# Float32 sums of key tiles ahead of one product for the last two groups of an attention and two-layer kernel

## The chip, the cores and the metric

The kernel runs on one core of one Trainium2 chip. The time is device microseconds (us) of that core for one execution; lower is better. Before the change it is 417.5 us, the median of three runs (417.23 to 418.01).

## The reference

Cosine attention over 8 batches, 12 heads, 448 positions and 64 columns per head, and behind it two matrix products with a leaky ReLU between them:

```python
q_n = q / (norm(q) + 1e-06);  k_n = k / (norm(k) + 1e-06)
scores = q_n @ k_n.T / tau                  # tau = 0.1
attn = exp(scores - max);  attn = attn / (sum(attn) + 1e-09)
x = (attn @ v) laid out as (3584 tokens, 768)
h = x @ w_in                                # 768 -> 2048
out = maximum(0.01 * h, h) @ w_out          # 2048 -> 768, float32
```

The kernel leaves the maximum out, since the scores are bounded by 1/tau. The softmax denominators are column sums of the exponentials, which TensorE forms as products with ones.

## The kernel before

**Engines.** TensorE (PE) does all products and a few transposes, ScalarE (ACT) the exponentials, logarithms and the leaky ReLU, VectorE (DVE) norms, normalisation, 32x32 transposes and copies out of PSUM, GpSimd (POOL) the squares of q and k and the loads of v and of the weights, SyncE (SP) the other transfers. The order of instructions on each engine is written out by hand: an engine runs its instructions in the order in which the program records them, and waits for others through semaphores.

**Heads.** Two heads make a pair; pair s has 0 to 47. Pairs 0 to 11 (the first two batches) go through an older form with four key tiles of 128, 128, 128 and 64 rows (`key_tiles`, `totals`, `products`, `scale`). The other 36 pairs go through `UNITS`: 18 units u of two pairs, each with seven key tiles i. A key tile is made by `quad_tiles`: eight 64x32 products (line 417) that each take an eighth of the array, into two PSUM banks, and one `exp` on ACT (line 423) into a buffer `pe` of 128 x 896 bf16, kept as `pq[u, i]`. Its 896 columns are two halves of 448 queries.

**Groups.** Units are gathered into ten groups g. The last two are group 8 (units 14 and 15) and group 9 (units 16 and 17). When all its key tiles are there, a group gets three passes of `group_products(g, e)` (line 442), each 7 key tiles x 4 strips x 2 row halves = 56 products of form 64x32 with 448 columns: e = None multiplies by `ones` and gives the denominators, e = 0 and 1 multiply by v (`vq`). `group_logs` takes the logarithm of the denominators (line 451), `group_inverse` the exponential of its negative (line 454), and `group_scale` on DVE (line 467) multiplies the v products by it into `xT`.

**Visits.** The 126 key tiles run in 42 visits of three (`visits`). A visit normalises one pair to come, makes its first tile, then one of a group's three passes if one is due (`parts`), then the other two tiles, and then some items of the feed-forward work: `first` (6 products with `w_in`, line 494, and the leaky ReLU on ACT, line 505) and `second` (16 products with `w_out`, line 531, a copy to `osb` by DVE, line 541, and a store by SP). A planner (`level`, `share`) deals these items out to visits so that each has about as much TensorE work. Group 8's ones pass falls in visit 38, its v passes in visits 39 and 40; group 9's come after the last visit, 41, with feed-forward items between them.

**Preparing pairs.** For a pair s: SP loads q or k (`load_qk`), POOL squares them (line 216), DVE sums (line 232), ACT takes roots (lines 245 and 246), DVE normalises (lines 253, 254 and 260) and transposes (line 306), and SP lays the result out as `qkT` in six transfers (line 315). `hold` is a one-element copy on POOL (line 616) that keeps POOL's queue behind DVE's normalisation. In the visits, `prepare` does this for the pair in `preps`; the last pair, 47, is prepared in visit 36.

**Before the visits.** Straight-line code takes care of pairs 6 to 14 and the first feed-forward chunk. `load_w_out(0)` and `load_w_out(1)` on POOL's queue load the two column halves of `w_out`, 1536 KB each (line 110). `settle(s)` normalises and transposes a pair, holds, and has the squares of a later pair made. `attend(j)` does the denominators, the products and the scaling of one quad of the older form.

**Memory.** `ps` is all of PSUM, eight banks dealt oldest first by `banks`. `vbp` holds three `v_b` buffers and `vrb` two remainders for the older form alone; `id128` is the identity for its transposes. `pep` has 25 `pe` buffers.

Of the kernel before, what the change touches and what calls it, by code (L numbers as in the profile page):

```python
# [8 lines left out]
F32 = mybir.dt.float32  # L9
BF16 = mybir.dt.bfloat16  # L10
AF = mybir.ActivationFunctionType
ALU = mybir.AluOpType
# [4 lines left out]
def kernel(  # L17
# [10 lines left out]
    nc = tc.nc  # L28
    B, H, S, D = q.shape
# [8 lines left out]
    NSLOT = B * NPAIR  # L38
    NQ = NPAIR // 2
    KT = D_model // 128  # L40
    MT = D_ff // 128
    HALF = D_model // 2
# [5 lines left out]
    ctx.enter_context(tc.manual_schedule())  # L48
    cpool = ctx.enter_context(tc.tile_pool(name="consts", bufs=1))
    ldp = ctx.enter_context(tc.tile_pool(name="ld", bufs=4))  # L50
    vbp = ctx.enter_context(tc.tile_pool(name="vb", bufs=3))
    smp = ctx.enter_context(tc.tile_pool(name="small", bufs=3))
    qnp = ctx.enter_context(tc.tile_pool(name="qn", bufs=3))
    ttp = ctx.enter_context(tc.tile_pool(name="tt", bufs=2))
# [11 lines left out]
    gp = nc.gpsimd  # L66
# [8 lines left out]
    def banks(count, keep=None):  # L75
        lo, hi = (0, 8) if not deals["apart"] else (0, 4) if count == 2 else (4, 8)
        x = min(
            (i for i in range(lo, hi, count) if not set(range(i, i + count)) & set(kept.values())),
            key=lambda i: max(age[i : i + count]),
        )  # L80
        deals["n"] += 1
        age[x : x + count] = [deals["n"]] * count
        if keep:
            kept[keep] = x
        return ps[:, x] if count == 1 else ps[:, x : x + count]
# [12 lines left out]
    w_out_sb = cpool.tile([128, MT, D_model], BF16, name="w_out_sb")  # L98
    w_in_r = moe_w_in.rearrange("(j p e) n -> e p j n", p=128, e=2)
    w_out_r = moe_w_out.rearrange("(mo mi) n -> mi mo n", mi=128)  # L100
# [4 lines left out]
            out=w_in_sb[:, e::2, n0 : n0 + D_ff // 2], in_=w_in_r[e, :, :, n0 : n0 + D_ff // 2]  # L105
        )

    def load_w_out(half):
        n0 = half * HALF
        gp.dma_start(out=w_out_sb[:, :, n0 : n0 + HALF], in_=w_out_r[:, :, n0 : n0 + HALF])  # L110

    def main(x, b, h0, nh):
        return x[b, h0 : h0 + nh, 0:MAIN].rearrange("h (p t) d -> p h t d", t=3)
# [28 lines left out]
    def load_qk(s):  # L142
        if s >= NSLOT:
            return
        whole = ldp.tile([128, 14 * D], F32, name="qk_h")
        if s >= OLD:
            u, which = divmod(s - OLD, 2)
            for w, pair in enumerate(UNITS[u][1]):
                b, h0 = pair // NPAIR, 2 * (pair % NPAIR)
                nc.sync.dma_start(  # L150
                    out=whole[64 * w : 64 * w + 64],
                    in_=(q, k)[which][b, h0 : h0 + 2].rearrange("h (p t) d -> (h p) (t d)", t=14),
                )
            raw[s] = whole
            return
        b, h0 = s // NPAIR, 2 * (s % NPAIR)
        q_h, k_h = halves(whole)
        nc.sync.dma_start(out=q_h[:, :, 0:3], in_=main(q, b, h0, 2))
        nc.sync.dma_start(out=k_h, in_=main(k, b, h0, 2))
        for i, x in enumerate((q, k)):  # L160
            nc.sync.dma_start(
                out=q_h[64 * i : 64 * i + 64, :, 3],
                in_=x[b, h0 : h0 + 2, MAIN:S].rearrange("h p d -> p h d"),
            )
        raw[s] = (q_h, k_h)
# [3 lines left out]
    vb, vrb = {}, []  # L169

    def load_v(j):
        if j >= B * NQ:
            return
        b, jj = divmod(j, NQ)
        vb[j] = vbp.tile([128, 4, 3, D], BF16, name="v_b")
        gp.dma_start(out=vb[j], in_=main(v, b, 4 * jj, 4))

    def load_v_rem(b, heads=range(4)):
# [7 lines left out]
    GROUPS = [(6,), (7, 8), (9, 10), (11,)] + [(j, j + 1) for j in range(12, 24, 2)]  # L186
# [2 lines left out]
        (g, (2 * js[0] + x, 2 * js[-1] + x if len(js) == 2 else 2 * js[0] + 1))  # L189
        for g, js in enumerate(GROUPS) for x in range(len(js))  # L190
    ]
    vq = {}

    def load_vq(g):
# [14 lines left out]
    def squares(s, eng=gp, parts=(0, 1)):  # L209
        if s >= NSLOT:  # L210
            return
        sq = sqt[s % 3]
        if s >= OLD:
            sqs[s] = sq
            x = raw[s].rearrange("p (t d) -> p t d", d=D)
            gp.tensor_tensor(sq[:, :, :D], x, x, op=ALU.mult)  # L216
            return
        sqs[s] = halves(sq.rearrange("p t d -> p (t d)"), D + 1)
        for i in parts:
            x, y = raw[s][i], sqs[s][i]  # L220
            if eng is nc.scalar:
                nc.scalar.activation(y[..., :D], x, func=AF.Square)
            else:
                eng.tensor_tensor(y[..., :D], x, x, op=ALU.mult)  # L224
# [23 lines left out]
    qn = {}  # L248
# [83 lines left out]
    def scores(s, kis):  # L332
        key_tiles([(s, ki) for ki in kis])
# [68 lines left out]
            given_back((j, e))  # L402

    pq = {}

    def quad_tiles(which):

# [19 lines left out]
    def group_products(g, e):  # L427


        us = [u for u, (gg, _) in enumerate(UNITS) if gg == g]  # L430
        two = len(us) == 2
        po = banks(2)
        for i in range(7):
            for strip in range(4):
                for w in range(2):
                    x, a = strip // 2, strip % 2
                    rows = slice(64 * w, 64 * w + 64)
                    weights = ones[rows] if e is None else (
                        vq[g][rows, strip if two else a, i]
                        .rearrange("p (d e) -> p e d", e=2)[:, e if two else w ^ x]  # L440
                    )
                    nc.tensor.matmul(  # L442
                        out=po[32 * strip : 32 * strip + 32, w, :S],
                        lhsT=weights, rhs=pq[us[x if two else 0], i][rows, a, :],
                        start=(i == 0), stop=(i == 6),
                    )
        return po
# [5 lines left out]
    def group_inverse(g):  # L453
        nc.scalar.activation(grb[g], grb[g], func=AF.Exp, scale=-1.0)
# [108 lines left out]
    def feed_groups(c, count):  # L563
        for _ in range(count):
            work[c].pop(0)[1]()
# [22 lines left out]
    nc.vector.memset(warm, 1.0)  # L588
    ones = cpool.tile([128, 32], BF16, name="ones")
    nc.vector.memset(ones, 1.0)  # L590
    ones_rem = cpool.tile([128, 2, 32], BF16, name="ones_rem")
    nc.vector.memset(ones_rem, 0.0)
    for i in range(2):
        nc.vector.memset(ones_rem[64 * i : 64 * i + 64, i], 1.0)
    for i in range(2):
        vrb.append(cpool.tile([128, NQ, 4, D], BF16, name=f"v_rem{i}"))
        nc.vector.memset(vrb[i], 0.0)
    id128 = cpool.tile([128, 128], BF16, name="id128")
    make_identity(nc, id128)
# [15 lines left out]
    def hold(x):  # L615
        gp.tensor_copy(out=seen, in_=x)  # L616
# [157 lines left out]
    hold(qn[s + 2][:, 6, 0, 0:1])  # L774
    squares(s + 4)
    load_v(s // 2 + 1)
    load_w_out(1)
    sums(s + 3)
    feed_groups(0, 2)
    scores(s + 1, (0, 1))  # L780
# [24 lines left out]
    def settle(s, more=()):  # L805
        normalise(s)
        if s >= OLD:
            transposes(s)
        hold(qn[s][:, 6, 0, 0:1])
        for x in (*more, s + 2):  # L810
            squares(x)
# [25 lines left out]

    scores(s + 4, (2,))
    scores(s + 5, (0, 1))
    feed_groups(0, 1)  # L840
    attend(NQ + 1)
    load_qk(s + 10)
    settle(s + 7)
    sums(s + 8)

    scores(s + 5, (2, 3))
# [40 lines left out]
        for n in range(len(visits))  # L887
    ]

    held = []  # L890
    fed = 0
    for n, tiles in enumerate(visits):
        s = preps.get(n, NSLOT)
        g, e = parts.get(n, (None, None))
        scaling = e is not None

        def prepare():
            if s < NSLOT:
                transposes(s)
                load_qk(s + 4)  # L900
                hold(qn[s][:, 6, 0, 0:1])
                squares(s + 2)
                sums(s + 1)

        normalise(s)
        if not scaling:
            prepare()
        quad_tiles(tiles[:1])
        if g is not None:
            po = group_products(g, e)  # L910
            if e is None:
                group_logs(g, po)
            else:
                group_scale(g, e, po)
        if scaling:
            prepare()
        quad_tiles(tiles[1:])
        if g is not None and e is None:
            group_inverse(g)
        for u, i in tiles:  # L920
            if i == 6 and u and UNITS[u][0] != UNITS[u - 1][0]:
                load_vq(UNITS[u][0])
        for c in marked:
            if at[c] == n:
                held += marked[c]
        level = min(
            (sum(loads[c] for c in loads if at[c] <= x) - fed + sum(side[n : x + 1])) / (x - n + 1)
            for x in range(n, len(visits))
        )
        share = (level - side[n]) / (4 if n == len(visits) - 1 else 1)  # L930
        now, done = [], 0
        while held:
            w = weight(held[0][0], held[0][1][0])
            if now and done + w / 2 > share:
                break
            now.append(held.pop(0)[1][1])
            done += w
        fed += done
        for fn in now[:-1]:
            fn()  # L940
        roots(s + 1)
        for fn in now[-1:]:
            fn()
    g = len(GROUPS) - 1
    group_logs(g, group_products(g, None))
    group_inverse(g)
    rest = [fn for _, (_, fn) in held]
    cut = len(rest) // 3
    for fn in rest[:cut]:
        fn()  # L950
    for e in range(2):
        group_scale(g, e, group_products(g, e))
# [39 lines left out]
```

## Time and profile before

| what | value |
|---|---|
| median of three runs | 417.5 us (417.23 to 418.01) |
| the profiled execution, its own time | 416.43 us |
| its span, first to last instruction | 414.6 us |
| granted TensorE clock over the span | 1.000 |
| ScalarE busy | 250.2 us, 60% |
| VectorE busy | 221.5 us, 53% |
| GpSimd busy | 114.6 us, 28% |
| denominators by ones (line 442, ones) | 560 matmuls in 10 passes |
| first-layer products (line 494) | 768 matmuls, 151.1 us |
| second-layer products (line 531) | 912 matmuls, 151.3 us |

The profile is of one execution, and its times are measured from the first instruction. Groups of instructions are named by line, engine, operation and out<-in tiles. PE is the matmul row, PEld the weight loads, which overlap it. A matmul's end is modelled from its size, so the starts say more than the durations: the recorded duration of a 64x32 matmul is 349 ns while 56 of them pass in 1.32 us. The chain of waits is the work that ended last, followed back from the last instruction; each of its steps has a start, a length and what ran.

### The profile page before, as it was taken

What the parts mean: (1) busy time and instruction counts of PE and PEld (TensorE: products, weight loads), DVE (VectorE), ACT (ScalarE), POOL (GpSimd) and SP (SyncE); (2) the same over time, 40 slices, a digit from 0 to 9 for tenths busy, and PEclk for the clock granted to TensorE, in tenths of its full rate; (3) what the DMA queues carried; (4) which work ended last, traced back from release to release, by engine and by line L of the source; (5) the groups of instructions that cost most, each with busy time, mean ns of one, the idle gap of its engine ahead of it and who ended that gap; (6) DMA issues with size and microseconds to landing.
All of it is one profiled execution on the core that took longest, in us unless ns stands there. A gap on an engine that the chain in (4) does not pass through costs nothing.

```text
span 414.6 us, 11342 instructions
## 1 busy us (share of the span) xinstructions
PE 407.1 (98%) x4799; PEld 212.3 (51%) x4799; DVE 221.5 (53%) x387; ACT 250.2 (60%) x431; POOL 114.6 (28%) x149
## 2 busy tenths in 40 slices
PE   8899999999999999999999999999999999999997
PEld 3335555544555555544455555554445555654565
DVE  6977976855778556766474964464621301210022
ACT  5997876378657785668865688547764464004300
POOL 4875543433234132413331433122210000000000
PEclk9999999999999999999999999999999999999999
DMA  7999998775377851884275681742442100020022
GB/s 195 242 214 220 210 234 187 181 223 129 60 206 182 204 132 22 204 229 99 53 186 157 151 229 43 175 126 84 91 90 68 51 39 3 38 77 0 2 76 76
DMA packets 41964, 53.82 MB, mean 130 GB/s; under 512 B 12474, under 2 KB 32314, under 8 KB 41914
## 3 DMA queue, kind: packets, MB, share of 16 engines
q1 hardware_dynamic: 25738, 41.01, 35.0%
q0 software_dynamic: 15488, 11.80, 19.7%
q8 instruction: 37, 0.61, 0.6%
q10 hardware_dynamic: 688, 0.30, 0.2%
q14 instruction: 13, 0.11, 0.1%
HBM read 45.61 MB, written 11.01 MB: 137 GB/s over the span
## 4 chain that ended last, share of the span: by engine, by line
PE 87%; DMA 4%; ACT 3%; DVE 3%; POOL 2%; SPq 1%; issue 1%; POOLq 0%
PE ps L531 34%; PE ps L494 34%; PE ps L442 9%; PE ps L417 7%; ACT pe L355 2%; DMA qk_h<-in_k_dram 2%; PE ps L366 2%; DVE qn L270 1%; DMA xT<-in_k_dram 1%; DMA xT<-in_q_dram 1%; POOL sq L224 1%; PE ps L346 1%; POOL sq L216 1%; DVE ss L238 0%; SPq L131 0%
## 5 line engine op out<-in xcount | busy, mean ns | idle before, releaser
L531 PE MATMUL ps<-w_out_sb,hT 128*128 128x384 bf16 (+1 forms) x912 | 151.3, 324 | 0.3 <-DVE xT L397 0.3
L494 PE MATMUL ps<-xT,w_in_sb 128*128 128x384 bf16 (+1 forms) x768 | 151.1, 353 | 0.0
L423 ACT ACTIVATE pe<-ps 128x896 bf16<-128x896 f32 x126 | 108.9, 915 | 46.1 <-PE ps L417 46.1
L531 PEld LDWEIGHTS <-hT 128*128 128x128 bf16 x912 | 86.5, 98 | 64.3 <-issue 10.0
L494 PEld LDWEIGHTS <-w_in_sb 128*128 128x128 bf16 x768 | 72.6, 98 | 74.3 <-issue 9.7
L505 ACT ACTIVATE hT<-ps 128x384 bf16<-128x384 f32 (+1 forms) x128 | 67.4, 552 | 56.0 <-PE ps L494 55.0
L541 DVE COPY osb<-ps 128x384 f32<-128x384 f32 (+1 forms) x57 | 31.2, 548 | 100.7 <-PE ps L531 100.6
L216 POOL TENSOR_TENSOR sq<-qk_h 128x896 f32<-128x896 f32 x36 | 61.0, 1695 | 9.2 <-DMA qk_h<-in_k_dram 7.7
L616 POOL CAST seen<-qn 128x1 f32<-128x1 bf16 x46 | 8.5, 185 | 169.4 <-DVE qn L260 160.5
L260 DVE TENSOR_TENSOR qn<-qk_h,r 128x896 bf16<-128x896 f32 x36 | 42.4, 1176 | 1.2
L232 DVE TENSOR_REDUCE ss<-sq 128x14 f32<-128x910 f32 x36 | 38.0, 1054 | 1.1 <-POOL sq L216 1.1
L355 ACT ACTIVATE pe<-ps 128x896 bf16<-128x896 f32 x42 | 35.9, 917 | 1.8 <-PE ps L346 1.7
L417 PE MATMUL ps<-qkT 64*32 64x448 bf16 x1008 | 36.5, 353 | 0.0
L253 DVE TENSOR_REDUCE r<-norms 128x14 f32<-128x28 f32 x48 | 8.6, 178 | 48.3 <-ACT norms L246 47.7
L467 DVE TENSOR_TENSOR xT<-ps,rb 128x448 bf16<-128x448 f32 x32 | 18.4, 617 | 23.2 <-PE ps L442 21.5
L306 DVE STREAM_TRANSPOSE tt<-qn 128x448 f32<-128x448 f32 x36 | 29.6, 821 | 0.9
L442 PE MATMUL ps<-pe,vq 64*32 64x448 bf16 x1008 | 27.0, 349 | 0.0
L245 ACT ACTIVATE ss<-ss 128x14 f32<-128x14 f32 x48 | 10.3, 214 | 25.4 <-DVE ss L232 24.4
L417 PEld LDWEIGHTS <-qkT 64*32 64x32 bf16 x1008 | 13.1, 91 | 19.2 <-issue 14.5
L442 PEld LDWEIGHTS <-vq 64*32 64x32 bf16 x1008 | 14.5, 92 | 8.0 <-issue 0.3
L442 PE MATMUL ps<-pe,ones 64*32 64x448 bf16 x560 | 15.1, 349 | 0.0
L346 PE MATMUL ps<-qkT 64*64 64x448 bf16 (+1 forms) x132 | 12.9, 359 | 2.1 <-ACT pe L355 1.2
(53 smaller groups left out, 218.9 us busy)
## 6 DMA issues: line engine op xcount, KB each, us to landing
qk_h<-in_q_dram SPq DMA_DIRECT2D x36, 224.0 KB, 4.0
qk_h<-in_k_dram SPq DMA_DIRECT2D x36, 224.0 KB, 4.3
out_dram<-osb SPq DMA_DIRECT2D x20, 384.0 KB, 2.3
qkT<-tt SPq DMA_DIRECT2D x72, 56.0 KB, 3.3
qkT<-tt SPq DMA_DIRECT2D x36, 112.0 KB, 3.5
vq<-in_v_dram POOLq DMA_DIRECT2D x16, 224.0 KB, 5.0
w_in_sb<-in_moe_w_in_dram POOLq DMA_DIRECT2D x4, 768.0 KB, 11.2
w_out_sb<-in_moe_w_out_dram POOLq DMA_DIRECT2D x2, 1536.0 KB, 22.3
```

Of the source, the lines that this page charges most:

```text
L216: gp.tensor_tensor(sq[:, :, :D], x, x, op=ALU.mult)
L232: nc.vector.tensor_reduce(ss[s], sqs[s], axis=AX.X, op=ALU.add)
L260: nc.vector.tensor_tensor(qn[s].rearrange("p m d e -> p m e d"), raw[s].rearrange(f"p ({t[1:-1]} d) -> p m e d", e=n, d=D), r.rearrange(f" ...
L306: nc.vector.transpose(out=to.rearrange(("p g (c m) -> p m g c", "p g (m c) -> p m g c")[which], m=7), in_=qn[s].bitcast(F32).rearrange("p ...
L355: nc.scalar.activation(out=dst, in_=sc[:, :, :S], func=AF.Exp, scale=inv_tau)
L417: nc.tensor.matmul(out=sc[32 * strip : 32 * strip + 32, a, :S], lhsT=x[rows, c0 : c0 + 32], rhs=x[rows, 0:S], start=True, stop=True,)
L423: nc.scalar.activation(out=pq[u, i], in_=sc[:, :, :S], func=AF.Exp, scale=inv_tau)
L442: nc.tensor.matmul(out=po[32 * strip : 32 * strip + 32, w, :S], lhsT=weights, rhs=pq[us[x if two else 0], i][rows, a, :], start=(i == 0), ...
L494: nc.tensor.matmul(out=pm[:, :n], lhsT=w_in_sb[:, kt, m * 128 : (m + 1) * 128], rhs=xT[c // 2][:, kt, c0 : c0 + n], start=(done + i == 0), ...
L505: nc.scalar.activation(out=hT[c][:, m, :n], in_=pm[:, :n], func=AF.Prelu, alpha=0.01)
L531: nc.tensor.matmul(out=po2[:, : hi - lo], lhsT=hT[c][:, m, ts * 128 : (ts + 1) * 128], rhs=w_out_sb[:, m, half * HALF + lo : half * HALF + ...
L541: nc.vector.tensor_copy(out=o[:, cols], in_=po2[:, : hi - lo])
```

## The change

Four edits stand in the diff.

1. For groups 8 and 9, the seven key tiles of each unit are added up element by element into one float32 tile of 128 x 896 (`whole[u]`), six additions a unit. GpSimd does unit 14, VectorE units 15, 16 and 17 (`add_up`). The ones pass of these two groups is then eight products of float32 `whole[u]` with float32 ones (`ones_f`) in place of 56 with bf16. VectorE's additions of a visit stand behind the visit's first feed-forward item; GpSimd's stand ahead of that visit's `hold` and `squares`. `group_inverse` of group 9 moves behind the first feed-forward item after its ones pass.
2. Two tiles of sums need room: `v_b` and `vrb` become views of one tile `shared`, whose space the sums take over once the older form is through with it, and `ones_f` is written over `id128` ahead of the visits.
3. The second half of `w_out` is loaded in two transfers of eight row blocks each.
4. Before the visits, the normalising, transposing and holding of pair 13, the load of pair 16 and the squares of pair 15 move ahead of one feed-forward item and `attend(NQ + 1)`, and with them their six `qkT` transfers on SP.

```diff
@@ -48,7 +48,6 @@
     ctx.enter_context(tc.manual_schedule())
     cpool = ctx.enter_context(tc.tile_pool(name="consts", bufs=1))
     ldp = ctx.enter_context(tc.tile_pool(name="ld", bufs=4))
-    vbp = ctx.enter_context(tc.tile_pool(name="vb", bufs=3))
     smp = ctx.enter_context(tc.tile_pool(name="small", bufs=3))
     qnp = ctx.enter_context(tc.tile_pool(name="qn", bufs=3))
     ttp = ctx.enter_context(tc.tile_pool(name="tt", bufs=2))
@@ -105,9 +104,13 @@
             out=w_in_sb[:, e::2, n0 : n0 + D_ff // 2], in_=w_in_r[e, :, :, n0 : n0 + D_ff // 2]
         )
 
-    def load_w_out(half):
-        n0 = half * HALF
-        gp.dma_start(out=w_out_sb[:, :, n0 : n0 + HALF], in_=w_out_r[:, :, n0 : n0 + HALF])
+    def load_w_out(half, pieces=1):
+        n0, step = half * HALF, MT // pieces
+        for m in range(0, MT, step):
+            gp.dma_start(
+                out=w_out_sb[:, m : m + step, n0 : n0 + HALF],
+                in_=w_out_r[:, m : m + step, n0 : n0 + HALF],
+            )
 
     def main(x, b, h0, nh):
         return x[b, h0 : h0 + nh, 0:MAIN].rearrange("h (p t) d -> p h t d", t=3)
@@ -172,7 +175,7 @@
         if j >= B * NQ:
             return
         b, jj = divmod(j, NQ)
-        vb[j] = vbp.tile([128, 4, 3, D], BF16, name="v_b")
+        vb[j] = v_old[:, j % 3]
         gp.dma_start(out=vb[j], in_=main(v, b, 4 * jj, 4))
 
     def load_v_rem(b, heads=range(4)):
@@ -189,6 +192,8 @@
         (g, (2 * js[0] + x, 2 * js[-1] + x if len(js) == 2 else 2 * js[0] + 1))
         for g, js in enumerate(GROUPS) for x in range(len(js))
     ]
+    ADDED = len(GROUPS) - 2
+    BY_VECTOR = len(UNITS) - 3
     vq = {}
 
     def load_vq(g):
@@ -402,6 +407,20 @@
             given_back((j, e))
 
     pq = {}
+    whole, due, summed = {}, [], set()
+
+    def add_up(eng):
+        for u, i in list(due):
+            if (gp if u < BY_VECTOR else nc.vector) is not eng:
+                continue
+            if i == 1:
+                if UNITS[u - 2][0] >= ADDED and UNITS[u - 2][0] not in summed:
+                    return
+                whole[u] = sum_of[u % 2]
+            due.remove((u, i))
+            eng.tensor_tensor(
+                whole[u], pq[u, 0] if i == 1 else whole[u], pq[u, i], op=ALU.add
+            )
 
     def quad_tiles(which):
 
@@ -430,6 +449,16 @@
         us = [u for u, (gg, _) in enumerate(UNITS) if gg == g]
         two = len(us) == 2
         po = banks(2)
+        if e is None and g >= ADDED:
+            summed.add(g)
+            for strip in range(4):
+                for w in range(2):
+                    rows = slice(64 * w, 64 * w + 64)
+                    nc.tensor.matmul(
+                        out=po[32 * strip : 32 * strip + 32, w, :S], lhsT=ones_f[rows],
+                        rhs=whole[us[strip // 2]][rows, strip % 2, :], start=True, stop=True,
+                    )
+            return po
         for i in range(7):
             for strip in range(4):
                 for w in range(2):
@@ -588,12 +617,19 @@
     nc.vector.memset(warm, 1.0)
     ones = cpool.tile([128, 32], BF16, name="ones")
     nc.vector.memset(ones, 1.0)
+    shared = cpool.tile([128, 3840], BF16, name="shared")
+    v_old = shared[:, :2304].rearrange("p (j h t d) -> p j h t d", j=3, t=3, d=D)
+    sum_of = [
+        shared[:, 1792 * i : 1792 * (i + 1)].bitcast(F32).rearrange("p (a c) -> p a c", c=S)
+        for i in range(2)
+    ]
     ones_rem = cpool.tile([128, 2, 32], BF16, name="ones_rem")
     nc.vector.memset(ones_rem, 0.0)
     for i in range(2):
         nc.vector.memset(ones_rem[64 * i : 64 * i + 64, i], 1.0)
     for i in range(2):
-        vrb.append(cpool.tile([128, NQ, 4, D], BF16, name=f"v_rem{i}"))
+        lo = 2304 + 768 * i
+        vrb.append(shared[:, lo : lo + 768].rearrange("p (j g d) -> p j g d", g=4, d=D))
         nc.vector.memset(vrb[i], 0.0)
     id128 = cpool.tile([128, 128], BF16, name="id128")
     make_identity(nc, id128)
@@ -774,7 +810,7 @@
     hold(qn[s + 2][:, 6, 0, 0:1])
     squares(s + 4)
     load_v(s // 2 + 1)
-    load_w_out(1)
+    load_w_out(1, 2)
     sums(s + 3)
     feed_groups(0, 2)
     scores(s + 1, (0, 1))
@@ -837,10 +873,13 @@
 
     scores(s + 4, (2,))
     scores(s + 5, (0, 1))
+    normalise(s + 7)
+    transposes(s + 7)
+    load_qk(s + 10)
+    hold(qn[s + 7][:, 6, 0, 0:1])
+    squares(s + 9)
     feed_groups(0, 1)
     attend(NQ + 1)
-    load_qk(s + 10)
-    settle(s + 7)
     sums(s + 8)
 
     scores(s + 5, (2, 3))
@@ -887,19 +926,23 @@
         for n in range(len(visits))
     ]
 
+    ones_f = id128.bitcast(F32)[:, 0:32]
+    nc.vector.memset(ones_f, 1.0)
     held = []
     fed = 0
     for n, tiles in enumerate(visits):
         s = preps.get(n, NSLOT)
         g, e = parts.get(n, (None, None))
         scaling = e is not None
+        adding = [(u, i) for u, i in tiles if i and UNITS[u][0] >= ADDED]
 
         def prepare():
             if s < NSLOT:
                 transposes(s)
                 load_qk(s + 4)
-                hold(qn[s][:, 6, 0, 0:1])
-                squares(s + 2)
+                if not adding:
+                    hold(qn[s][:, 6, 0, 0:1])
+                    squares(s + 2)
                 sums(s + 1)
 
         normalise(s)
@@ -915,6 +958,11 @@
         if scaling:
             prepare()
         quad_tiles(tiles[1:])
+        due += adding
+        add_up(gp)
+        if adding and s < NSLOT:
+            hold(qn[s][:, 6, 0, 0:1])
+            squares(s + 2)
         if g is not None and e is None:
             group_inverse(g)
         for u, i in tiles:
@@ -936,17 +984,22 @@
             now.append(held.pop(0)[1][1])
             done += w
         fed += done
-        for fn in now[:-1]:
+        for fn in now[:1]:
+            fn()
+        add_up(nc.vector)
+        for fn in now[1:-1]:
             fn()
         roots(s + 1)
-        for fn in now[-1:]:
+        for fn in now[1:][-1:]:
             fn()
     g = len(GROUPS) - 1
     group_logs(g, group_products(g, None))
-    group_inverse(g)
     rest = [fn for _, (_, fn) in held]
     cut = len(rest) // 3
-    for fn in rest[:cut]:
+    for fn in rest[:1]:
+        fn()
+    group_inverse(g)
+    for fn in rest[1:cut]:
         fn()
     for e in range(2):
         group_scale(g, e, group_products(g, e))
```

## The prediction

> **What bounds the kernel now.** I read the page's busy shares first, then the chain of waits around the two ones passes, then what the other engines wait for there.
>
> ```profile
> PE 407.1 (98%) x4799; PEld 212.3 (51%) x4799; DVE 221.5 (53%) x387; ACT 250.2 (60%) x431; POOL 114.6 (28%) x149
> ...
> 314.36 0.31 PE ps L417 x8
> 314.67 1.32 PE ps L442 x56
> 315.99 0.38 PE ps L417 x16
> ...
> 334.41 9.86 PE ps L494 x60
> 344.27 1.45 PE ps L442 x56
> 345.71 4.01 PE ps L494 x24
> ```
>
> The first line gives busy us, share and count by engine; the others are steps of the chain (start, length, what). TensorE is at 98%, and from about 80 us to 411 us every step of the chain is a TensorE step, each beginning where the last one ended. So TensorE's own instruction time sets the end: a microsecond taken out of its stream or put into it is a microsecond of span. The two L442 steps shown are the ones passes of groups 8 (visit 38) and 9 (after visit 41).
>
> How do 56 matmuls pass in 1.32 us? Three stretches of group 9's ones pass, with the matmuls in flight in brackets behind the PE busy time:
>
> ```profile
> 344.19:344.23 0.04, 0.03 (x8) 0.03 (x10) 1.00 0.00 0
> ...
> 344.23:344.39 0.16, 0.16 (x8) 0.10 (x16) 1.00 0.00 0
> ...
> 344.39:344.43 0.04, 0.04 (x16) 0.03 (x8) 1.00 0.00 0
> ```
>
> Eight start within 0.04 us; for the next 0.16 us none starts; then eight more start within 0.04 us. The eight of a round sit on eight different parts of the array and run side by side. The ninth needs the first one's part, waits until that is free, and everything recorded behind it waits too. A round, or wave, costs 1.32 / 7 = 0.189 us.
>
> **The float32 product.** This is the term that decides. Per group 56 matmuls go, 7 waves, 1.32 us. Eight float32 products come. The built program holds 4719 matmuls and 4719 weight loads where the old one holds 4799 of each: 80 fewer, so the 112 bf16 matmuls that went were replaced by 32. Each of the 16 float32 products has become two weight loads and two matmuls, recorded one behind the other, on the same part of the array, and only then comes the next product's part.
>
> No float32 matmul is in the trace, so its cost is bounded. The nearest row is the wave of 0.189 us for 448 columns. If a float32 matmul cost one wave and all eight parts ran side by side, a pass would be near 0.19 us (a gain of 1.13 a group); if every one of the 16 matmuls ran alone and took two waves, it would be 16 x 0.378 = 6.05 us (a loss of 4.73 a group). I take two waves for one matmul: an element has twice the bits, and two matmuls that are to give the full product of halves times halves must each cover both halves of the moving side, so 0.378 us. And I take the order from the windows above: the second matmul of a product finds its part taken by the first and holds back all behind it; when it starts, the next product's first one, on another part, starts right behind it. So there is one step of 0.378 us per product and one more at the end: 9 x 0.378 = 3.40 us. Against 1.32 us that is +2.08 us a group, **+4.16 us** for two. The second weight load of a product is taken as hidden behind its first matmul, as 98 ns loads are behind the 163 ns matmuls of L531; if it isn't, 16 x 0.093 us (the recorded load of a 64x32 part) adds 1.5 us.
>
> The Trainium skill, "FP8 and Floating Point Precision", section TensorE Precision Notes, says that true FP32 takes four passes through the array; two matmuls of two waves are these four, and no run here shows it yet. The skill's "TensorEngine Tiling (Array Packing)", section Key Properties, says that different tiles can execute weight loads and matmuls in parallel. By that rule alone the eight products would overlap in full, 4 x 0.189 = 0.76 us a pass, and the sum would be a gain of 1.13 us in place of the loss; the rounds of eight above agree with it only for parts that are called in turn, which these are not.
>
> **The additions.** VectorE gets 18, GpSimd 6, each over 128 x 896. The nearest rows:
>
> ```profile
> L216 POOL TENSOR_TENSOR sq<-qk_h 128x896 f32<-128x896 f32 x36 | 61.0, 1695 | 9.2 <-DMA qk_h<-in_k_dram 7.7
> ...
> L260 DVE TENSOR_TENSOR qn<-qk_h,r 128x896 bf16<-128x896 f32 x36 | 42.4, 1176 | 1.2
> ...
> 333.83 0.56 DVE L541 COPY osb<-ps 128x384 f32<-128x384 f32 x1 [1.90 <-PE ps L531]
> 351.30 2.41 DVE L467 TENSOR_TENSOR xT<-ps,rb 128x448 bf16<-128x448 f32 x4 [16.92 <-PE ps L442]
> ```
>
> At 1.18 us, VectorE's are 18 x 1.18 = 21.2 us, at 1.70 us GpSimd's 6 x 1.70 = 10.2 us. Off the path, if they end before the product that reads them. Group 9: unit 17's six additions stand behind the copy at 333.83, so 334.39 + 6 x 1.18 = 341.5, against the product at 344.27: 2.8 us to spare, and VectorE had 16.9 us idle there. Group 8: its last addition, tile (15, 6), stands behind the copy that starts at 311.79, so it ends at 312.35 + 1.18 = 313.5 against 314.67, 1.1 us to spare. Queued behind the additions on VectorE are `osb` copies and `group_scale`; TensorE meets those only when it wants their banks back, and a copy of three additions' length (3.5 us) later is still inside a visit of 5 to 7 us. On GpSimd the additions of unit 14 wait for the exponentials of visits 33 and 34 and push two squares and one load of v back by some 5 us: squares of pair 46 would end at about 286 instead of 282, and the sums that read them ran at 291.10; the load of v has some 17 us left. Cost 0; without this cover it is a wait at the products, priced as a rival.
>
> **The rest.** The ring of 25 `pe` buffers, `shared` and `ones_f` cost TensorE nothing: their earlier readers are long done. `group_inverse` behind one more activation (0.49 us) still ends some 3 us before the scaling at 351.30. One short memset joins VectorE at 80 us.
>
> ```profile
> PEld L531 <- DMA w_out_sb<-in_moe_w_out_dram: 0.7, 1, 0.7
> ...
> 70.49 5.38 PE L531 MATMUL ps<-w_out_sb,hT 128*128 128x384 bf16 x32 [0.26 <-DVE xT L397]
> ```
>
> The second half of `w_out` is issued at 49.12 and lands in some 21 us, just when line 531 wants it at 70.49. The weight load waits for this transfer, so the 0.26 us of idle TensorE is its work (the bank that the matmul takes was copied out at 67.94). In two transfers, the first piece of 768 KB lands far earlier (`w_in`'s of that size take 11.2 us), and the second one is wanted 8 matmuls, 1.3 us, later. That takes out **-0.26 us**; for 0.4 us more of issue on GpSimd, ahead of a `hold` that sat idle 1.88 us. It can cost something only if the second piece lands 1.3 us later than the whole did.
>
> Pair 13's preparation moves ahead of a feed-forward copy and of `attend`'s scaling. Its roots are there at 66.33, so VectorE normalises and transposes until 68.7, copies until 69.3 and still reaches the scaling, which waits for ACT until 69.82: cost 0. On SP the six `qkT` transfers (3.77 us of issue) pass ahead of pair 16's load, which goes from 63.26 to about 72.6; with the 7 us that loads took there it lands at about 80, 3 us later than GpSimd's squares of it began (76.67), while the sums that read them began at 83.71. Cost 0. The gain is that pair 13's `qkT` lands about 4 us earlier than its use at 80.95: cover, not time.
>
> **The sum.** +4.16 - 0.26 = **+3.9 us** on the profiled execution's 416.43 us (span 414.6 and 1.8 around it): 420.3. The median of the runs is 1.07 above that execution, so **421.4 us**.
>
> **Rivals.**
> - *All eight parts overlap* (the other side, faster): if a product's second matmul queued at its own part and let others pass, a pass would be four waves, 0.76 us, and two save 1.13. With the 0.26: -1.39, 416.1 us. For it: eight parts do run side by side. Against it: nothing started in the 0.16 us shown although the ninth alone lacked its part. It decides as soon as two passes take less than 2.9 us together.
> - *One wave each, in that order*: 9 x 0.189 = 1.70 us a pass, +0.76 - 0.26 = +0.5, 418.0 us. For it: a bf16 matmul of 448 columns costs that. Against: twice the bits.
> - *Nothing overlaps*: 6.05 us a pass, +9.46 - 0.26 = +9.2, 426.7 us. For it: no float32 matmul of this form is in the trace, and its weight loads might block all parts.
> - *Late additions*: they hold the product of group 9 from (344.27 - 334.39) / 6 = 1.65 us each on. At 2.16 us, GpSimd's slowest square, six end at 347.4: up to 3 us on top, 424.4. Against: VectorE's row is 1.18.
>
> **Chances.** The forecast (3.4 us a pass, weights hidden or not) 0.57, full overlap 0.27, one wave each 0.05, nothing overlaps 0.08, late additions 0.03. About 0.2%, 0.84 us, is what a measurement can tell from no change; full overlap is faster by more, one wave each is within it, the others are slower: 0.27, 0.05, 0.68. The forecast's own range is 420.3 to 423.0 (the 1.5 us of weight loads on top). The range runs from a little below full overlap, 415.6, to 423.0; it leaves out the case without overlap and the worst of the late additions.
>
> **What would show it.** In the chain, the two float32 passes at 3.4 us each, 16 matmuls in steps of about 0.38 us: right. At 0.8 us: the order on the array was misread. At 6 us: no overlap. The additions should be near 1.2 us on VectorE and 1.7 us on GpSimd, with no TensorE wait for either. The wait on `w_out` at 70 us should be gone. An idle gap of TensorE ahead of a float32 product, or new waits on `qkT` near 81 us, would make the additions or the moves the story instead.

## The result, and the profile after

The changed kernel takes 418.31 us (median of 22 runs, 417.31 to 420.95) against 417.23 for the one before (22 runs). The ratio is 1.0021 with a 95% interval of 1.0011 to 1.0031: slower by 0.9 us, not by the 3.9 us that were forecast. The profiled execution took 418.29 us, with a span of 416.5 us against 414.6.

The page's first line, and the chain of waits around the two float32 passes (line 457; lines 436, 523 and 560 are the former 417, 494 and 531):

```profile
PE 407.3 (98%) x4719; PEld 211.4 (51%) x4719; DVE 240.0 (58%) x406; ACT 250.2 (60%) x431; POOL 126.0 (30%) x156
...
315.73 0.31 PE ps L436 x8
316.04 0.75 PE ps L457 x16
316.79 0.38 PE ps L436 x16
...
324.20 0.77 issue
324.98 0.56 DVE osb L570
325.54 0.04 issue
325.58 0.48 PE ps L436 x7
...
336.78 9.86 PE ps L523 x60
346.63 0.91 PE ps L457 x16
347.55 4.01 PE ps L523 x24
```

The float32 passes did not get longer, they got shorter: 0.75 us instead of 1.32, and 0.91 instead of 1.45. But in visit 39 a step of VectorE has come into the chain, where every step had been TensorE's. VectorE's order there shows why:

```profile
319.98 0.56 DVE L570 COPY osb<-ps 128x384 f32<-128x384 f32 x1 [3.66 <-PE ps L560]
320.46 1.08 DVE L421 TENSOR_TENSOR shared<-pe 128x896 f32<-128x896 bf16 x1
321.57 3.48 DVE L421 TENSOR_TENSOR shared<-shared,pe 128x896 f32<-128x896 f32 x3
324.98 0.55 DVE L570 COPY osb<-ps 128x384 f32<-128x384 f32 x1
```

Unit 16's sums take over unit 14's space, so its first addition has to wait for group 8's pass in visit 38, and then four additions stand in a row. The copy behind them starts at 324.98; before, the same copy started at 321.71, 2.5 us behind the one ahead of it instead of 5.0. TensorE's tiles of visit 39 want that bank. The same copy before, and the start of visit 39's tiles and of its first feed-forward item in the chain before:

```profile
321.71 0.56 DVE L541 COPY osb<-ps 128x384 f32<-128x384 f32 x1 [1.97 <-PE ps L531]
```

```profile
321.68 0.31 PE ps L417 x8
...
323.69 5.31 PE ps L531 x32
```

There is a second loss, much earlier. Here are the waits of TensorE after 48 us (in total, times, longest), then GpSimd's order at the two transfers of `w_out`'s second half (start, length, engine, line, what, and in brackets the idle time before), then its squares before:

```profile
PE ps L436 <- DVE osb L570: 1.1, 1, 1.1
PE ps L289 <- DVE qn L275: 0.6, 1, 0.6
PE ps L351 <- DVE qkT L330: 0.4, 1, 0.4
```

```profile
48.24 0.90 POOL L110 DMA_DIRECT2D w_out_sb<-in_moe_w_out_dram  x1
53.07 0.87 POOL L110 DMA_DIRECT2D w_out_sb<-in_moe_w_out_dram  x1 [3.93 <-DVE qkT L330]
53.94 0.20 POOL L652 CAST seen<-qn 128x1 f32<-128x1 bf16 x1
54.08 1.82 POOL L229 TENSOR_TENSOR sq<-qk_h 128x512 f32<-128x512 f32 x2
```

```profile
52.31 1.82 POOL L224 TENSOR_TENSOR sq<-qk_h 128x512 f32<-128x512 f32 x2
```

GpSimd stood still for 3.9 us ahead of the second transfer, so the squares behind it began at 54.08 instead of 52.31, and sums, roots and normalisation of pair 11 came after them. (The view names VectorE's copy of `qkT` as what ended this wait, since that came last by the profile; the second experiment shows that it was something else.) TensorE waited 0.6 us for its transpose at 58 us and 0.4 us for `qkT` at 62 us.

Added up over the two profiled executions, by when the same step begins: 1.4 us later by line 560's item at 71.86 (70.49 before), 0.57 won in visit 38, 1.56 lost in visit 39 (from the start of its tiles to its first feed-forward item 3.58 us instead of 2.02), 0.54 won at group 9's pass: +1.4 - 0.57 + 1.56 - 0.54 = +1.85, the span's 1.9. Single executions differ by more than the effect (before: 416.27 to 419.89), so sizes below are ratios of runs, and the trace says only where.

### The profile page after: what moved, and what is told of

It is laid out like the page before. It is cut to its first block, busy times and chain, and to the rows that moved or that the text cites. A ratio compares the mean times of both kernels' runs of the same rounds, so it can differ in the third digit from the quotient of the medians.

```text
span 416.5 us, 11224 instructions
## 1 busy us (share of the span) xinstructions
PE 407.3 (98%) x4719; PEld 211.4 (51%) x4719; DVE 240.0 (58%) x406; ACT 250.2 (60%) x431; POOL 126.0 (30%) x156
## 4 chain that ended last, share of the span: by engine, by line
PE 92%; ACT 3%; DVE 2%; POOL 1%; issue 1%; DVEq 0%; POOLq 0%
PE ps L523 35%; PE ps L560 35%; PE ps L471 8%; PE ps L436 7%; PE ps L371 2%; ACT pe L360 2%; PE ps L641 2%; PE ps L351 2%; PE ps L289 1%; DVE qn L275 1%; DVE qkT L330 0%; PE ps L457 0%; POOL sq L221 0%; POOL sq L229 0%; DVE ss L243 0%
## 5 line engine op out<-in xcount | busy, mean ns | idle before, releaser
L265 DVE TENSOR_TENSOR qn<-qk_h,r 128x896 bf16<-128x896 f32 x36 | 43.8, 1218 | 1.2
L421 DVE TENSOR_TENSOR shared<-shared,pe 128x896 f32<-128x896 f32 x15 | 16.3, 1088 | 1.2
```

What stands on the lines that cost most here:

```text
L265: nc.vector.tensor_tensor(qn[s].rearrange("p m d e -> p m e d"), raw[s].rearrange(f"p ({t[1:-1]} d) -> p m e d", e=n, d=D), r.rearrange(f" ...
```

## The experiments

Five questions: does the early loss come from the two transfers, does the loss in visit 39 come from the additions in a row, does the move of pair 13 do anything, how does TensorE let eight float32 products overlap, and what does the float32 form still cost.

**One transfer again**, in the changed kernel.

```diff
-    load_w_out(1, 2)
+    load_w_out(1)
```

> The changed kernel with the second half of w_out in one transfer again, all else kept. Theory (the second of the two transfers waits on GpSimd for the landing of the first half of w_out, 3.9 us, and holds back the squares of the next pair): the two TensorE gaps between 57 and 63 us go (1.8 us) and the wait of 0.3 us at line 531's first use of the second half comes back, so about 1.4 us less than the changed kernel: near 416.9 us, ratio to before 0.999. Rival (the gaps come from the moved preparation of pair 13 or from the shared tile): no better than the changed kernel, 418.3, and the gaps stay.

Measured: 416.64 us, ratio to before 0.9982 (0.9972 to 0.9992). The gaps at 58 and 62 us are gone; the wait of 1.1 us in visit 39 stays. But no wait on `w_out` came back at 70 us, which the theory had counted on; the runs on the move, below, take that up.

**The two transfers alone**, in the kernel before.

> The kernel before with nothing but the two transfers for the second half of w_out. Theory (semaphore wait of the second transfer): GpSimd idle near 4 us ahead of it, TensorE 1.4 us later after 70 us, about 418.6 us, ratio 1.0035. Rival (the moved preparation or the shared tile is the cause): 0.3 us gained, about 417.0 us, ratio 0.999.

Measured: 418.0 us, ratio 1.0013 (1.0004 to 1.0023): slower, with neither sums nor move in it, though less than expected. Its wait of GpSimd is named outright:

```profile
POOL w_out_sb L111 <- DMA w_out_sb<-in_moe_w_out_dram: 2.4, 1, 2.4
```

The second transfer waits for another transfer of `w_out`: its first half. In the built program, and in the traces, GpSimd's loads take eight semaphores in turn, and the second transfer's turn falls on the one that `load_w_out(0)` has still to raise. In the changed kernel's trace that first half was issued at 29.44 us and landed at 52.79. In the three traces with the stall (the changed kernel, this one, and the one with two additions below) the second transfer starts 0.28 us after that landing: 53.07 after 52.79, 53.88 after 53.60, 53.28 after 53.00. The wait is 2.4 us here and 3.9 there, since in this execution TensorE sat idle for 1.35 us at 20 us already and GpSimd arrived later; so the loss differs from one execution to the next. The loss is also smaller here because, without the move, the two transfers still have a wait on `w_out` to take out: this trace has none at 70 us, where the kernel before has one. That share was not measured by itself. VectorE's copy of `qkT`, named above, is not what the transfer waits for: here and with two additions it ends 0.5 to 0.7 us after the transfer has started.

**At most two additions in a row**, in the changed kernel.

```diff
-    def add_up(eng):
+    def add_up(eng, most=99):
         for u, i in list(due):
+            if not most:
+                return
...
+            most -= 1
...
-        add_up(nc.vector)
+        add_up(nc.vector, 2 if 38 <= n < 41 else 99)
```

> The changed kernel with at most two VectorE additions between two items of feed-forward work in visits 38 to 40 (the others wait for the next visit). Theory (four additions in a row in visit 38 hold back the copy of a bank that the tiles of visit 39 need): the TensorE wait of 1.1 us in visit 39 goes and its 0.5 us around it too, about 1.5 us less than the changed kernel: 416.8 us, ratio 0.999. Rival (the bank is late because of the float32 product or of the group's scaling): the wait stays, 418.3 us.

Measured: 416.92 us, ratio 0.9987 (0.9978 to 0.9996). TensorE has no wait left after 300 us, and VectorE's copy is back at 2.6 us behind the last one:

```profile
320.20 0.56 DVE L573 COPY osb<-ps 128x384 f32<-128x384 f32 x1 [3.66 <-PE ps L563]
320.67 1.08 DVE L424 TENSOR_TENSOR shared<-pe 128x896 f32<-128x896 bf16 x1
321.79 1.09 DVE L424 TENSOR_TENSOR shared<-shared,pe 128x896 f32<-128x896 f32 x1
322.80 0.55 DVE L573 COPY osb<-ps 128x384 f32<-128x384 f32 x1
```

**Both undone** (one transfer, two additions), float32 passes kept.

> The changed kernel with the second half of w_out in one transfer and at most two VectorE additions in a row in visits 38 to 40: both losses out, the float32 passes kept. Theory (two independent waits of 1.4 to 1.6 us hid a gain of 0.55 us a pass): the two ratios found singly add up, 1.0021 - 0.0039 - 0.0034 = 0.995, 415.0 us, and no TensorE wait over 0.3 us is left behind 52 us. Rival (one loss only moves the other, as with a later wait for qkT or a bank): 0.997 or more, 416.0 us.

Measured: 415.26 us, ratio 0.9949 (0.9933 to 0.9966), as the two single effects add up. TensorE has no wait left after 48 us. This is 1.0021 - 0.9949 = 0.7%, 3.0 us, below the changed kernel and faster than the one before.

**The second transfer later**: the same with two transfers, the second behind pair 11's squares.

```diff
...
-    load_w_out(1)
+    load_w_out(1, 2, (0,))
...
     squares(s + 5)
+    load_w_out(1, 2, (1,))
     load_v(s // 2 + 2)
```

> As the kernel with both undone, but w_out's second half in two transfers again, the second of them issued 5 us later, behind the squares of pair 11 and ahead of the load of v. Theory (the stall is the semaphore that the second transfer shares with w_out's first half, which lands at about 52.7 us): GpSimd no longer idles ahead of it, the squares are as early as with one transfer, and the wait of 0.3 us on w_out at 70 us goes: 0.1 to 0.3 us less than one transfer, ratio 0.994 to 0.995. Rival (two transfers cost in themselves, by more issue or by slower landing): a wait for the second piece at 71 us, 0.996 or more.

Measured: 415.62 us, ratio 0.9957 (0.9941 to 0.9973). The stall is gone, so it was the place and not the splitting. The hoped-for 0.1 to 0.3 us didn't come: its interval holds the one-transfer kernel's ratio, and that kernel had no wait on `w_out` left to remove.

**Without the move** (both undone, fourth edit undone too, so the sums alone), **the move alone** in the kernel before, and **the move without its load** (both undone, pair 16's load back at its old time on SP, the rest of the move kept):

```diff
+    load_qk(s + 10)
     normalise(s + 7)
     transposes(s + 7)
-    load_qk(s + 10)
```

> As the kernel with both undone, and pair 13's preparation, pair 16's load and pair 15's squares back in their old place. The prediction put the move at no time: same as with the move, 0.995. Rival (the move makes qkT of pair 13 land in time for the first visit at 81 us, now that the stages before it are shorter): a TensorE wait of 0.2 to 1 us at about 81 us, 0.996 to 0.997.

> The kernel before with nothing but the fourth edit: pair 13's preparation, pair 16's load and pair 15's squares moved ahead. Theory (it takes q of pair 16 out of the transfers beside w_out's second half, which then lands in 20.0 instead of 21.3 to 22.1 us, before line 531 wants it at 70.2 us): the wait of 0.3 to 1.0 us there goes, ratio 0.998 to 0.999. Rival (the prediction's: the move is cover alone): 1.000.

> As the kernel with both undone, but pair 16's load stands ahead of pair 13's preparation, so that SP issues it at about 63 us again; the work of VectorE and GpSimd stays moved. Theory (this load is what delays w_out's landing): the wait on w_out at 70 us is back with 0.3 to 1.0 us, ratio 0.996 to 0.997, as without the move (0.9972). Rival (the earlier VectorE work is what helps): 0.995, no wait at 70 us.

Measured: 0.9972 (0.9961 to 0.9983) without the move, 0.9983 (0.9973 to 0.9994) for the move alone, 0.9978 (0.9966 to 0.9991) with the load in its old place. The wait that came back without the move, and then with the load alone put back, is in both cases on `w_out`, not on `qkT`:

```profile
70.89 5.37 PE L563 MATMUL ps<-w_out_sb,hT 128*128 128x384 bf16 x32 [1.00 <-DMA w_out_sb<-in_moe_w_out_dram]
```

```profile
71.51 1.80 PE L563 MATMUL ps<-w_out_sb,hT 128*128 128x384 bf16 x10 [1.22 <-DMA w_out_sb<-in_moe_w_out_dram]
```

Nine of the profiled kernels load `w_out`'s second half in one transfer. In five of them pair 16's load goes out on SP at 63 to 65 us, and in four of these TensorE waited on `w_out` at 70 us: 0.26 us (before), 1.00 (without the move), 1.22 (load in its old place) and 0.95 (four in a row, below), but not with seven in a row. In the other four the load goes out at 73 to 74 us (one transfer, both undone, the move alone, and the sum rounded to bf16, below), and there is no such wait. So it is the load's place on SP that pays: 0.17% or 0.7 us by the move alone, 0.23% or 1.0 us from 0.9972 to 0.9949. The intervals of 0.9949 with the load moved and 0.9978 without meet at 0.9966.

How it pays is less sure than the theory has it. From issue to landing the second half took 20.6 to 22.1 us in the five, 21.5 on the mean, and 20.0 to 21.3 in the four, 20.5 on the mean: some 1 us apart, in ranges that overlap. With the move alone it took 21.3 us, as long as before. There the wait is gone because GpSimd issued the transfer 1.2 us earlier (47.88 instead of 49.12) while TensorE wanted it only 0.4 us earlier (69.80 instead of 70.23).

**Seven in a row, and four in a row**: the bf16 ones passes of the kernel before, recorded part by part.

```diff
+        order = [(i, strip, w) for i in range(7) for strip in range(4) for w in range(2)]
+        if e is None and g >= len(GROUPS) - 2:
+            order.sort(key=lambda x: (x[1], x[2], x[0]))             # seven in a row
+            order.sort(key=lambda x: (x[0] // 4, x[1], x[2], x[0]))  # or: four, then three
+        for i, strip, w in order:
...
```

> The kernel before, with the 56 bf16 matmuls of the ones passes of groups 8 and 9 recorded part by part: seven for one part of the array in a row, then seven for the next. By the prediction's reading (a matmul whose part is taken holds back everything behind it) a pass is 8 x 7 - 7 = 49 waves of 0.189 us, 9.3 us instead of 1.3, and the span grows by 15.9 us. Rival (it waits at its own part and others pass, as the float32 pass of 0.75 us suggests): a pass stays near 1.3 to 1.5 us and the span at 414.6 us. In between, if only a few can wait at a time: several us a pass.

> The kernel before, with the 56 bf16 matmuls of the ones passes of groups 8 and 9 recorded four for one part in a row, then four for the next, and then the last three tiles in rows of three. Theory (up to three matmuls can wait at their own part while others pass, read from seven in a row, where the next part's first one starts with the fourth): a pass stays near 1.3 to 1.6 us, the span near 414.6 us. Rival (three can wait in all, whatever their part): parts follow each other in twos as with seven in a row, some 4 us a pass, the span 5 us longer.

The chain's step for group 9's pass, with seven in a row, and with four:

```profile
349.12 5.51 PE ps L443 x56
```

```profile
345.25 1.77 PE ps L443 x56
```

Seven in a row cost 5.5 us, neither the 9.3 of a strict order nor the 1.45 of free overlap. In the starts of that trace the fourth matmul of a part and the first of the next begin 6 ns apart: the next part gets its turn when the last three of the part before are left waiting. That makes a part every three waves, 7 x 3 + 7 = 28 waves or 5.3 us. Four in a row leave three waiting from the beginning, and the pass costs only 0.32 us more than in the old order; the spans were 423.6 and 416.0 us, of one execution each, so the reading rests on the pass and not on the span. So up to three matmuls wait at their own part while others pass. It isn't three in all: of the float32 pass, eight wait at once, one at each part:

```profile
315.85:315.89 0.04, 0.03 (x8) 0.03 (x8) 1.00 0.20 77
315.89:316.22 0.33, 0.33 (x8) 0.10 (x8) 1.00 1.11 410
316.22:316.27 0.05, 0.05 (x16) 0.00 (x0) 1.00 0.98 246
```

These are three stretches of group 8's float32 pass in the changed kernel, with the matmuls in flight in the first brackets and the weight loads in the second. Recorded as first and second matmul of one product after the other, eight start at once all the same, and eight more 0.37 us later. So the second matmul of a product let the first ones of the next products pass.

**The sum rounded to bf16**, both losses undone.

```diff
+            to = sum_bf[u % 2] if i == 6 else whole[u]
             eng.tensor_tensor(
-                whole[u], pq[u, 0] if i == 1 else whole[u], pq[u, i], op=ALU.add
+                to, pq[u, 0] if i == 1 else whole[u], pq[u, i], op=ALU.add
             )
+            whole[u] = to
...
-                        lhsT=ones_f[rows],
+                        lhsT=ones[rows],
```

> As the kernel with both undone, but the last addition of each unit writes bf16, so that the eight products of a pass are bf16 (the sum is rounded to bf16). Theory (a float32 pass is four waves, 0.75 us, a bf16 one a single wave of 0.19 us, all on the path): 0.56 us less for each of two passes, 1.1 us less, ratio 0.9923, 414.0 us. Rival (the pass is bound by drains and waits around it, not by its waves): 0.3 us less or nothing.

Measured: 414.81 us, ratio 0.9936 (0.992 to 0.9953), the fastest of all; against the float32 one it is 0.13%, 0.5 us, half of what was expected, and the intervals overlap. The chain shows where the half went:

```profile
314.40 0.36 PE ps L441 x8
314.76 0.02 issue
314.79 0.93 ACT pe L447
315.71 0.04 issue
315.76 5.36 PE ps L565 x32
...
343.71 0.31 PE ps L462 x8
```

Group 9's pass is down to 0.31 us on the path, from 0.91. In visit 38 the pass has become so short that the first feed-forward item waits for ScalarE's exponential to give a bank back: there the gain is not TensorE's to keep.

## Why the prediction was right and wrong

**The float32 product, +4.16 us: wrong, in its order.** The size of one matmul was right: 448 float32 columns take two waves (second round 0.37 us behind the first). The step that failed is "holds back all behind it": the second matmul of a product waited at its own part, and the next product's first one started at once. The windows of before showed eight starts, a pause and eight starts, and that is what both readings give when parts are called in turn: nothing behind the ninth could have started much earlier than it did. Seven and four in a row are the test that the trace of before didn't hold. With waiting at the own part the pass is four waves, 0.75 us against the rival's price of 0.76, and the two passes gained 0.57 and 0.54 us where a loss of 2.08 each was forecast. The Trainium skill's "TensorEngine Tiling (Array Packing)", section Key Properties, which says that different tiles can execute weight loads and matmuls in parallel, was set aside for the row and was the better guide. These runs agree with it as long as no more than three matmuls wait at a part.

**The two transfers, -0.26 us: wrong in sign.** The wait at 70 us that they were to take out was real, though 0.26 us was its length in one execution: with the same load on SP it was between nothing and 1.22 us in five. But "0.4 us more of issue on GpSimd, ahead of a `hold` that sat idle 1.88 us" counted the second transfer's issue and not its wait for a semaphore. Undoing it is worth 1.0021 - 0.9982 = 0.39%, 1.6 us.

**The additions, 0: near enough in their durations, wrong in one place.** VectorE's took 1.08 to 1.09 us (1.18 taken), GpSimd's 1.9 (1.70 taken), its first 2.5. Both products found their sums ready (they ended at 314.7 and 343.7, the passes began at 316.0 and 346.6), and the squares and the load of v pushed back on GpSimd cost no wait of TensorE. What failed is "a copy of three additions' length (3.5 us) later is still inside a visit": it was four additions, since unit 16 has to wait for unit 14's space, and the bank was wanted inside that time. Worth 1.0021 - 0.9987 = 0.34%, 1.4 us.

**The move, 0: wrong, through a part that was priced from its own side only.** Pair 16's load later was counted as a later landing of that load; what the runs show is that with the load later the wait on `w_out` is gone. It is gone in the trace of the move alone, so the two transfers had nothing left to win.

That the sum came out on the forecast side is luck. The passes gained 1.1 us (the sums alone, without the move: 1 - 0.9972 = 0.28%, 1.2 us) and the move 0.7 to 1.0, two waits cost 1.6 and 1.4 us: 0.9 to 1.2 us slower in all, where 0.9 was measured, and none of these four terms is the one that was forecast.

## What to carry to other kernels

Before a transfer is cut in two, look up which semaphore its second part will wait for, and what stands behind it on that queue; here, a few us later on the same queue, it was free. Additions that one engine takes over belong where no copy that frees a bank is queued behind them, so ask how many can become ready at once. A row that fits a theory is no evidence for it if the rival predicts the same row: here matmuls called part by part in turn said nothing on what a waiting matmul does to those behind it.

## What the runs showed of the hardware

- A float32 product of 448 columns on a 64x32 part is two weight loads and two matmuls of 0.37 us each; eight on eight parts take 0.75 us together, with the seconds of all eight waiting at their parts.
- Up to three bf16 matmuls waited at their own part while those of other parts passed; the fourth held back all behind it (1.77 us a pass with four in a row, 5.51 with seven, 1.45 in turn).
- A GpSimd addition of two bf16 tiles into float32, 128 x 896, took 2.50 us; with one float32 operand 1.89; its float32 squares of that size 1.68. VectorE took 1.08 and 1.09 us for the same two additions.
- A load of 1536 KB landed in 20.6 to 22.1 us in five runs with a load of 448 KB (q of one unit) issued 13 to 16 us behind it, and in 20.0 to 21.3 us in four without: some 1 us apart on the mean, with ranges that overlap.
- GpSimd's loads take eight semaphores in turn: in three runs a transfer waited 2.4 to 3.9 us on that queue for one issued 23 us earlier that had its semaphore.
